# Squared-ReLU attention with expert routing: the 64-key tail tile of each chunk in one score product instead of two

## The chip, the cores and the metric

The kernel runs on one core of a Trainium2 chip. The metric is the device time of one execution in microseconds (us). The engines are PE (TensorE, matmuls; PEld is its weight load), ACT (ScalarE), DVE (VectorE), POOL (GpSimd) and SP (SyncE, which issues most DMAs). Each has its own queue of instructions; semaphores order them across engines.

## The reference, cut to what matters

```python
scores = (1.0 / S) * np.matmul(z, z.transpose(0, 2, 1))
attn = np.maximum(scores, 0.0) ** 2
x = (u * np.matmul(attn, v)).reshape(B * S, D)
# each row of x goes to one of 4 x 4 experts, chosen by two argmax steps
h = np.maximum(x_e @ w1[e], 0.0)
out = weight * (h @ w2[e])
```

B is 8 batches, S 1856 tokens, D 256 features; z has 64 features. All inputs are fp32. There are 16 experts with 1024 hidden units each.

## The kernel before, in words

**Precision.** A product of fp32 numbers is built from fp32r parts: a number is split into a rounded high part and the low rest, and high x low products are added. ACT writes the high part (a cast), DVE subtracts it from the original to get the low part. z has only 64 features, so each z tile holds z twice, in partitions 0 to 63 and 64 to 127. `z2h` is the high part of both copies, `z2l` the low part of both (`split_z`, L269; `prep_z`, L251, for later batches). The query side `zm` (`prep_zm`, L301) holds the high part in its upper 64 partitions and the low part in its lower 64. One product `z2h` x `zm` thus gives high x high + high x low, and `z2l` x `zm` gives the rest.

**Attention.** For every batch the queries come in four chunks of 512, 512, 320 and 512 columns (`QW`). A chunk has 15 key steps (`NK`): 14 full tiles of 128 keys and the tail of 64. `scores` (L342) makes the scores of one step: two products into one PSUM bank out of three (L349, L350), a Relu by ACT (L352), a square by ACT (L358), the rounding to the high part by DVE (L359) and the low part by DVE (L362). In steps 4 and 10 of a chunk (`ACT_TWICE`) ACT makes the high part with a second square instead (L355, L356). `attn_v` (L370) multiplies with the values: six products a step (L381, L382, L384), into two banks of accumulators. Scores run five steps (`LEAD`) ahead of it.

**The tail step before.** The 64 tail keys are loaded twice side by side (L279 to L281 and `prep_z`), so that `z2h` and `z2l` have 128 columns for this step and its scores stand in all 128 partitions, twice. DVE then keeps the high part in the upper 64 partitions and overwrites the lower 64 with the low part (L365); the values of the tail stand twice as well, and four products finish the step.

**After a chunk.** `chunk_end` (L392) gates with u (L402, DVE), splits the result (L403 ACT, L404 DVE), and defers the rest to later steps: `logits` (L435), four PE products for the router and a transpose by DMA; `planes` (L417), ACT copies whose 16-bit halves go through four transposes on SP into `rows`; `logits_tr` (L450). `route` (L483) is a chain of some twenty small DVE operations, three a step, which ends in a scatter of the rows to their experts by POOL. It updates `base`, the experts' fill counts (L566). The router uses a single PSUM bank (`ps_m`) for logits and for ranks.

**Loads and splits.** `PREP` (L930) says at which (chunk, step) each quarter of the next batch's v and z is loaded and at which it is split. In the last batch `E0_LOADS`, `E0_CUTS`, `E1_LOADS` and `E1_CUTS` (L934 to L937) do the same for the weights of the first two experts, in four pieces each; the last piece of expert 1 is split by `start_piece` (L1250) in the expert stage. z tiles and the logits' planes share two buffers (tag `zr`).

**Order.** The first 15 steps (`NHELD`) and the expert stage run in the order in which they are written, on PE, ACT, DVE and SP. The steps between are ordered by a planner that simulates the engines and gives each the oldest instruction that it takes to be ready; an instruction marked `held` (L186) stays behind what was traced before it on its engine. Each engine's order is fixed when the kernel is built.

**Experts.** `up` (L764) and `down` (L778) work through blocks of up to 512 rows, eight groups of products a block. The first block's products are woven into the last attention steps.

## Time and profile before

| | |
|---|---|
| median of 3 runs | 1507.86 us (1505.93 to 1508.85) |
| the profiled execution | 1506.0 us |
| its span, first to last instruction | 1504.2 us |
| PE busy | 1488.0 us, 7607 matmuls |
| DVE, ACT busy | 1102.7 us, 996.0 us |
| POOL busy | 298.6 us |
| end of attention, start of the expert stage | some 840 us into the span |

The span starts with the first instruction of the program. In rows of a timeline the first number is the start in us, the second the duration in us; a wait stands in brackets behind, with what ended it. A matmul's duration runs until its result is written and overlaps with the next ones, so that the distance of two starts is what one costs. In rows of groups the numbers behind the bar are busy time in us and the mean duration in ns, and behind the second bar the idle time of the engine just before.

### The profile page before, as it was taken

The page shows a single profiled execution, that of the slowest core. Times are in us where ns is not written, and L with a number is a line of the kernel's source. Part 1 is how long each engine was busy: PE and PEld are TensorE (multiplying, and loading weights), DVE is VectorE, ACT ScalarE, POOL GpSimd, SP SyncE. Part 2 cuts the span into 40 slices and gives each one's busy share as a digit, 9 for nine tenths or more (in the row PEclk, how much of TensorE's full clock was granted, in tenths as well). Part 3 has the DMA queues.
Part 4 walks back from the last instruction along what each step waited for, and adds up shares of the span by engine and source line. Part 5 has one row for each costly group of instructions (what it writes and reads, how often), then busy time and mean ns, then how long its engine had stood idle before and what let it go on. Part 6 is the DMA issues. An engine that isn't in the chain of part 4 may idle for free. (4 is left out here: it accounts for less than half of the span.)

```text
span 1504.2 us, 23839 instructions
## 1 busy us (share of the span) xinstructions
PE 1488.0 (99%) x7607; PEld 1297.4 (86%) x7607; DVE 1102.7 (73%) x2619; ACT 996.0 (66%) x1885; POOL 298.6 (20%) x343
## 2 busy tenths in 40 slices
PE   9999999999999999999999999999999999999997
PEld 7888888888888888888888799999888899889996
DVE  7888888888787888788798656665665556666663
ACT  8888888888888888888788435444444444444442
POOL 0012121121202121211103122321222222222222
PEclk9999999999999999999999999999999999999999
DMA  4323423333335244332574384866545665767641
GB/s 137 106 73 110 97 74 102 88 85 91 97 78 113 61 114 85 75 83 73 155 235 127 90 154 101 161 142 138 111 87 114 142 135 138 134 140 135 135 94 50
DMA packets 303588, 167.76 MB, mean 112 GB/s; under 512 B 239467, under 2 KB 282477, under 8 KB 303216
## 3 DMA queue, kind: packets, MB, share of 16 engines
q1 hardware_dynamic: 290896, 132.63, 40.5%
q0 software_dynamic: 11968, 30.91, 6.8%
q14 instruction: 277, 2.27, 0.6%
q8 instruction: 95, 1.56, 0.5%
q10 hardware_dynamic: 352, 0.39, 0.1%
HBM read 72.51 MB, written 41.60 MB: 76 GB/s over the span
## 5 line engine op out<-in xcount | busy, mean ns | idle before, releaser
L773 ACT ACTIVATE hh<-ph 128x512 fp32r<-128x512 f32 (+7 forms) x296 | 150.2, 515 | 318.1 <-PE ph L771 240.8
L381 PE MATMUL o<-ah,vl 128*128 128x512 f32 (+1 forms) x960 | 354.5, 371 | 0.6 <-DVE ah L359 0.4
L382 PE MATMUL o<-ah,vh 128*128 128x512 f32 (+1 forms) x960 | 354.4, 371 | 0.0
L774 DVE SCALAR_TENSOR_TENSOR hl<-ph,hh 128x512 fp32r<-128x512 f32 (+7 forms) x296 | 169.9, 581 | 224.3 <-ACT hh L773 213.7
L362 DVE TENSOR_TENSOR al<-r,ah 128x512 fp32r<-128x512 f32 (+1 forms) x448 | 285.5, 638 | 51.5 <-ACT r L356 42.8
L352 ACT ACTIVATE r<-sc 128x512 f32<-128x512 f32 (+1 forms) x480 | 260.1, 552 | 94.4 <-PE sc L350 69.3
L384 PE MATMUL o<-al,vh 128*128 128x512 f32 (+1 forms) x896 | 295.4, 372 | 0.0
L358 ACT ACTIVATE r<-r 128x512 f32<-128x512 f32 (+1 forms) x416 | 240.9, 592 | 6.1
L576 POOL DMA_INDIRECT bucket<-rows,di x120 | 130.4, 1087 | 538.6 <-issue 217.5
L789 POOL DMA_INDIRECT out_dram<-yf,meta x129 | 144.1, 1117 | 458.3 <-DVE yf L833 411.7
L769 PE MATMUL ph<-xh_m,w1l_e 128*128 128x512 f32 (+7 forms) x592 | 205.5, 347 | 1.3 <-issue 1.3
L771 PE MATMUL ph<-xl_m,w1h_e 128*128 128x512 f32 (+7 forms) x592 | 205.5, 347 | 0.3 <-DVE xl_m L750 0.2
L381 PEld LDWEIGHTS o<-ah,vl 128*128 128x128 f32 x960 | 180.5, 188 | 28.8 <-DVE vl L299 0.6
L770 PE MATMUL ph<-xh_m,w1h_e 128*128 128x512 f32 (+7 forms) x592 | 205.1, 346 | 0.0
L382 PEld LDWEIGHTS o<-ah,vh 128*128 128x128 f32 x960 | 180.5, 188 | 27.3
L786 PE MATMUL y<-hl,w_e 128*128 128x512 f32 (+7 forms) x576 | 200.5, 348 | 0.4 <-DVE hl L774 0.4
L784 PE MATMUL y<-hh,w_e 128*128 128x512 f32 (+7 forms) x576 | 200.1, 347 | 0.0
L785 PE MATMUL y<-hh,w_e 128*128 128x512 f32 (+7 forms) x576 | 200.0, 347 | 0.0
L359 DVE CAST ah<-r 128x512 fp32r<-128x512 f32 (+1 forms) x416 | 166.1, 400 | 37.0 <-ACT r L358 35.5
L384 PEld LDWEIGHTS o<-al,vh 128*128 128x128 f32 x896 | 165.3, 188 | 27.5 <-DVE al L362 0.4
L349 PE MATMUL sc<-zm,z2h 128*128 128x512 f32 (+1 forms) x480 | 179.9, 375 | 0.0
L350 PE MATMUL sc<-zm,z2l 128*128 128x512 f32 (+1 forms) x480 | 177.7, 371 | 0.0
(148 smaller groups left out, 2056.3 us busy)
## 6 DMA issues: line engine op xcount, KB each, us to landing
raw_e<-in_w_dram SPq DMA_DIRECT2D x64, 512.0 KB
ut<-in_uT_dram SPq DMA_DIRECT2D x24, 512.0 KB
vr<-in_v_dram SPq DMA_DIRECT2D x23, 512.0 KB
bucket<-padrow SPq DMA_DIRECT2D x16, 528.0 KB
zr<-in_zT_dram SPq DMA_DIRECT2D x47, 128.0 KB
ut<-in_uT_dram SPq DMA_DIRECT2D x8, 320.0 KB
vr<-in_v_dram SPq DMA_DIRECT2D x9, 256.0 KB
out_dram<-yf,meta POOLq DMA_INDIRECT x129, 3.2
```

The source lines that it names most:

```text
L352: nc.scalar.activation(out=a, in_=ps[:, 0:w], func=AF.Relu, scale=1.0 / S)
L358: nc.scalar.activation(out=a, in_=a, func=AF.Square)
L362: nc.vector.tensor_sub(out=al, in0=a, in1=f32(ah))
L381: nc.tensor.matmul(o, vl[:, dsl], ah, start=(k == 0), stop=False)
L382: newest[:] = [nc.tensor.matmul(o, vh[:, dsl], ah, start=False, stop=(k == NK - 1))]
L384: nc.tensor.matmul(o, vh[:, dsl], al, start=False, stop=False)
L769: nc.tensor.matmul(o, wt["l"][d][:, fs], xh[:, d, 0:W], start=(d == 0), stop=False)
L770: nc.tensor.matmul(o, wt["h"][d][:, fs], xh[:, d, 0:W], start=False, stop=False)
L771: nc.tensor.matmul(o, wt["h"][d][:, fs], xl[:, d, 0:W], start=False, stop=(d == ND - 1))
L784: nc.tensor.matmul(o, w2t[:, 1, dsl], hh[:, 0:W], start=(f == 0), stop=False)
L785: nc.tensor.matmul(o, w2t[:, 0, dsl], hh[:, 0:W], start=False, stop=False)
L786: nc.tensor.matmul(o, w2t[:, 0, dsl], hl_[:, 0:W], start=False, stop=(f == NF - 1))
```

## The change

The tail tile is no longer loaded twice. Its `z2h` columns get the high part in the first 64 and the low part, made by one more DVE subtract, in the second 64. One product with `zm` then gives partial sums in partitions 0 to 63 (from the high part) and 64 to 127 (from the low part). ACT copies the second half to partitions 0 to 63 of an SBUF tile, DVE adds the first half from PSUM, and Relu, square and rounding run on 64 partitions; the low part is written into partitions 64 to 127 from there. In the 320-wide chunk ACT now squares twice in steps 8, 10 and 12 instead of 4 and 10. The second half of the gating in `chunk_end` is deferred by a step, and the two `planes` from steps 3 and 4 to 6 and 8 behind the chunk, except in the last batch. The tables of loads and splits get other times, with one of their own for the first batch, and the third weight piece of expert 1 is split in the expert stage.

```diff
-    ACT_TWICE = (4, 10)
+    ACT_TWICE = ((4, 10), (8, 10, 12))
...
     def prep_z(b, c):
...
-        for h in range(2):
-            nc.sync.dma_start(zr[h * DQ:(h + 1) * DQ, 0:w], zT[b, :, q0:q0 + w])
-            if wx > w:
-                nc.sync.dma_start(zr[h * DQ:(h + 1) * DQ, w:wx], zT[b, :, S - TAIL:S])
...
+        load_z(b, c, zr, (nc.sync, nc.sync))
+        return lambda: split_z(b, c, zr)
 
     def split_z(b, c, zr):
...
+        w = ZW[c]
         z2h, z2l = new_z(f"z2h_{b}_{c}"), new_z(f"z2l_{b}_{c}")
...
+        ins = nc.scalar.copy(out=z2h[:, 0:w], in_=zr[:, 0:w])
+        if b > 0:
+            held(ins)
+        nc.vector.tensor_sub(out=z2l[:, 0:w], in0=zr[:, 0:w], in1=f32(z2h[:, 0:w]))
+        if c == NQ - 1:
+            tail = slice(w - TAIL, w)
+            nc.vector.tensor_sub(out=z2h[:, w:w + TAIL], in0=zr[:, tail], in1=f32(z2h[:, tail]))
...
     def load_z(b, c, zr, queues):
...
-            if c == NQ - 1:
-                queues[h].dma_start(zr[h * DQ:(h + 1) * DQ, w:w + TAIL], zT[b, :, S - TAIL:S])
...
     def scores(s):
...
-        nc.tensor.matmul(ps[:, 0:w], z2h[:, ks], zm, start=True, stop=False)
-        nc.tensor.matmul(ps[:, 0:w], z2l[:, ks], zm, start=False, stop=True)
+        nc.tensor.matmul(ps[:, 0:w], z2h[:, ks], zm, start=True, stop=k == NKF)
         a = sb("r", [P, 512], F32, 4, f"r_{s}")[:, 0:w]
-        nc.scalar.activation(out=a, in_=ps[:, 0:w], func=AF.Relu, scale=1.0 / S)
+        if k < NKF:
+            nc.tensor.matmul(ps[:, 0:w], z2l[:, ks], zm, start=False, stop=True)
+            nc.scalar.activation(out=a, in_=ps[:, 0:w], func=AF.Relu, scale=1.0 / S)
+        else:
+            a = a[0:TAIL]
+            nc.scalar.copy(out=a, in_=ps[TAIL:P, 0:w])
+            nc.vector.tensor_add(out=a, in0=ps[0:TAIL, 0:w], in1=a)
+            nc.scalar.activation(out=a, in_=a, func=AF.Relu, scale=1.0 / S)
         ah = new_z(f"ah_{s}")[:, 0:w]
-        if k in ACT_TWICE:
+        if k in ACT_TWICE[w == min(QW)]:
...
-            nc.vector.tensor_copy(out=ah, in_=a)
+            nc.vector.tensor_copy(out=ah[0:a.shape[0]], in_=a)
...
-            nc.vector.tensor_sub(out=ah[TAIL:P, :], in0=a[TAIL:P, :], in1=f32(ah[TAIL:P, :]))
+            nc.vector.tensor_sub(out=ah[TAIL:P, :], in0=a, in1=f32(ah[0:TAIL, :]))
...
     def chunk_end(s):
...
-        for d in range(ND):
+
+        def gate(d):
             nc.vector.tensor_mul(out=xT[:, d, :], in0=oa[d][:, 0:w], in1=u_t[:, d, :])
...
+        gate(0)
+        if b + 1 == B:
+            gate(1)
+        else:
+            defer(s + 1, lambda: gate(1))
...
-        defer(s + 3, lambda: planes(0))
-        defer(s + 4, lambda: planes(1))
+        defer(s + (3 if b + 1 == B else 6), lambda: planes(0))
+        defer(s + (4 if b + 1 == B else 8), lambda: planes(1))
...
     PREP = (
-        ("v", 0, (0, 1), (0, 6)), ("v", 1, (0, 7), (0, 12)), ("v", 2, (0, 13), (1, 4)), ("v", 3, (1, 5), (1, 10)),
-        ("z", 0, (1, 7), (1, 13)), ("z", 1, (2, 5), (2, 11)), ("z", 2, (3, 5), (3, 11)), ("z", 3, (3, 6), (3, 13)),
+        ("v", 0, (0, 1), (0, 5)), ("v", 1, (0, 6), (0, 11)), ("v", 2, (0, 12), (1, 3)), ("v", 3, (1, 4), (1, 7)),
+        ("z", 0, (1, 5), (1, 9)), ("z", 1, (2, 13), (3, 5)), ("z", 2, (3, 4), (3, 9)), ("z", 3, (3, 7), (3, 12)),
     )
-    E0_LOADS = ((1, 4), (1, 5), (1, 12), (2, 0))
-    E0_CUTS = ((1, 11), (1, 14), (2, 5), (2, 9))
-    E1_LOADS = ((2, 9), (2, 13), (3, 7), (3, 11))
-    E1_CUTS = ((3, 6), (3, 9), (3, 13))
+    PREP0 = (
+        ("v", 0, (0, 6), (0, 11)), ("v", 1, (0, 7), (0, 12)), ("v", 2, (0, 13), (1, 4)), ("v", 3, (1, 5), (1, 8)),
+        ("z", 0, (1, 6), (1, 10)), ("z", 1, (2, 13), (3, 5)), ("z", 2, (3, 4), (3, 9)), ("z", 3, (3, 7), (3, 12)),
+    )
+    E0_LOADS = ((1, 4), (1, 5), (1, 9), (1, 12))
+    E0_CUTS = ((1, 8), (1, 11), (1, 13), (3, 1))
+    E1_LOADS = ((2, 9), (3, 2), (3, 8), (3, 11))
+    E1_CUTS = ((3, 7), (3, 10))
...
-    def start_piece():
-        add_w(wts[1], 3, "e1")
-        e1_cuts[3]()
-
-    then(5, start_piece)
+    def start_piece(pc):
+        add_w(wts[1], pc, "e1")
+        e1_cuts[pc]()
+
+    then(3, lambda: start_piece(2))
+    then(5, lambda: start_piece(3))
```

`w == min(QW)` is true in the 320-wide chunk and picks the second entry of `ACT_TWICE`. `PREP0` is used in the first batch; `PREP` before had one exception for it, v 0 at (0, 6) and (0, 11).

## Rows read from the trace of the kernel before

**Rows 1.** The page: span, busy time by engine, and one costly group.
```profile
span 1504.2 us, 23839 instructions
...
PE 1488.0 (99%) x7607; PEld 1297.4 (86%) x7607; DVE 1102.7 (73%) x2619; ACT 996.0 (66%) x1885; POOL 298.6 (20%) x343
...
L381 PE MATMUL o<-ah,vl 128*128 128x512 f32 (+1 forms) x960 | 354.5, 371 | 0.6 <-DVE ah L359 0.4
```

**Rows 2.** Busy time by stretches of the span; the last line sums the first 850 us.
```profile
core 0: us, PE busy (x) PEld busy (x) DVE busy (x) ACT busy (x) POOL busy (x), PEclk, DMA share, GB/s
...
50.00:250.00 200.00, 200.00 (x980) 168.66 (x979) 166.74 (x480) 170.20 (x323) 33.76 (x40) 1.00 0.35 91
...
sum 850.00, PE 845.29 PEld 709.37 DVE 704.63 ACT 704.74 POOL 140.17; mean PE 120.76 PEld 101.34 DVE 100.66 ACT 100.68 POOL 20.02
```

**Rows 3.** Timeline of PE in batch 3: first and last of fifteen starts.
```profile
334.80 0.39 PE L349 MATMUL sc<-zm,z2h 128*128 128x512 f32 x1
...
337.97 0.39 PE L350 MATMUL sc<-zm,z2l 128*128 128x512 f32 x1
```

**Rows 4.** Timeline of PE, last batch: first and last of thirteen narrow starts, then scores.
```profile
798.02 0.31 PE L381 MATMUL o<-ah,vl 128*128 128x320 f32 x1
...
799.78 0.31 PE L381 MATMUL o<-ah,vl 128*128 128x320 f32 x1
...
800.37 0.39 PE L349 MATMUL sc<-zm,z2h 128*128 128x512 f32 x1
```

**Rows 5.** Groups by line and shape, ACT and DVE.
```profile
L352 ACT ACTIVATE r<-sc 128x512 f32<-128x512 f32 x360 | 210.1, 591 | 69.9 <-PE sc L350 54.5 <-DVE al L362 7.9 <-PE pk L557 1.4
...
L352 ACT ACTIVATE r<-sc 128x320 f32<-128x320 f32 x120 | 50.1, 435 | 24.5 <-PE sc L350 14.8 <-DVE al L362 8.2 <-DVE ah L365 1.4
...
L359 DVE CAST ah<-r 128x320 fp32r<-128x320 f32 x104 | 34.3, 330 | 4.9 <-ACT r L358 4.2 <-PE sc L350 0.7
...
L402 DVE TENSOR_TENSOR xT<-o,ut 128x512 f32<-128x512 f32 x48 | 31.9, 683 | 0.2
...
L402 DVE TENSOR_TENSOR xT<-o,ut 128x320 f32<-128x320 f32 x16 | 7.6, 481 | 0.0
...
L355 ACT ACTIVATE ah<-r 128x320 fp32r<-128x320 f32 x16 | 7.5, 470 | 0.0
...
L455 DVE TENSOR_TENSOR lg<-lgf 128x80 f32<-128x80 f32 x24 | 5.7, 236 | 0.2
```

**Rows 6.** Waits: who waited for whom, total us, times, longest us.
```profile
DVE al L362 <- ACT r L356: 42.8, 34, 2.4
```

**Rows 7.** Timeline of batch 3: the tail step of the 320-wide chunk.
```profile
384.12 0.31 PE L350 MATMUL sc<-zm,z2l 128*128 128x320 f32 x1
...
385.94 0.44 ACT L352 ACTIVATE r<-sc 128x320 f32<-128x320 f32 x1 [1.08 <-DVE al L362]
...
389.15 0.49 DVE L365 TENSOR_TENSOR ah<-r,ah 64x320 fp32r<-64x320 f32 x1
...
392.64 0.30 PE L381 MATMUL o<-ah,vl 128*128 128x320 f32 x1
```

**Rows 8.** Timeline around the end of attention.
```profile
830.44 0.69 DVE L214 TENSOR_TENSOR w_e<-raw_e,w_e 128x512 fp32r<-128x512 f32 x1
...
841.29 0.47 PE L438 MATMUL pl<-xh,whl 128*128 128x512 f32 x1 [2.82 <-DVE base L566]
...
842.26 1.05 ACT L748 CAST xh_m<-xf 128x1024 fp32r<-128x1024 f32 x1 [2.14 <-PE pl L438]
...
844.74 0.69 DVE L774 SCALAR_TENSOR_TENSOR hl<-ph,hh 128x512 fp32r<-128x512 f32 x1 [2.68 <-ACT hh L773]
```

**Rows 9.** Timeline of the last batch: the tail step of the 320-wide chunk.
```profile
801.11 0.35 DVE L452 COPY lgf<-lgx 128x320 uint16<-128x320 uint16 x1 [1.56 <-DMA lgx<-lgp]
...
801.49 0.49 DVE L365 TENSOR_TENSOR ah<-r,ah 64x320 fp32r<-64x320 f32 x1
...
802.05 0.40 PE L381 MATMUL o<-ah,vl 128*128 128x320 f32 x1
```

More of the change, by code (lines that the diff above doesn't have):

```diff
@@ L972, in step @@
         if b + 1 < B:
-            for what, n, load, cut in PREP:
-                if b == 0 and (what, n) == ("v", 0):
-                    load, cut = (0, 6), (0, 11)
+            for what, n, load, cut in PREP if b else PREP0:
                 if (c, k) == load:
```

12 lines of the change are left out of this document (removed).

## The prediction

> **What bounds the kernel now.** I read the page first: the profiled execution has a span of 1504.2 us and took 1506.0 us with what lies around the span; the median of the runs shown is 1507.86 us, 1.9 us above that execution. TensorE (PE) is busy for 99% of the span [rows 1], which alone proves little, since matmul ends are modelled. So I looked for waits: the product that a late split would hold up, L381, sat idle 0.6 us in all of its 960 instances [rows 1]. The view by stretches says the same of the attention stage: in each 200 us PE is busy 200.00 us at a granted clock of 1.00, ScalarE (ACT) 170 us and VectorE (DVE) 167 us [rows 2]. The timeline shows what "busy" is worth: from 334.80 to 337.97 us fifteen 512-wide products start, fourteen steps of 0.226 us without a hole [rows 3]; the 320-wide ones start every (799.78 - 798.02) / 12 = 0.147 us [rows 4]. In attention, then, PE's number of products sets the time, and the other engines have some 15% to spare. The one large hole of the stage is its end, 2.82 us [rows 8].
>
> **The products removed.** The last key tile of each chunk loses its second score product. There are 8 x 4 = 32 chunks, 24 of 512 queries and 8 of 320: 24 x 0.226 + 8 x 0.147 = 5.4 + 1.2 = **6.6 us** less on PE. Nothing lies beside these slots: PE is the engine without holes, so they come off the path whole, as long as what follows is ready in time. [...]
>
> **What the tail step gains on ACT and DVE.** ACT copies 64 partitions out of PSUM, 24 x 0.591 + 8 x 0.435 us by the Relu that reads the same bank; DVE adds the halves, 24 x 0.683 + 8 x 0.481 us by the multiply that reads PSUM and SBUF; eight 64-wide subtracts for z, at most 0.236 us each [rows 5]. I take rows on 128 partitions for work on 64: the subtract on 64 partitions takes 0.49 us for 320 columns [rows 7], the multiply on 128 takes 0.481 [rows 5]. With three doubled squares instead of two in the 320-wide chunk, ACT gets 8 x 0.470 more and DVE loses 8 x 0.330 [rows 5]. Sums: ACT 17.7 + 3.8 = +21.5 us, DVE 20.2 + 1.9 - 2.6 = +19.5 us. In the first 850 us they are busy 704.74 and 704.63 us [rows 2], so both go to some 726 of 843, 86%. Cost on the path: zero, hidden under PE. If that cover were gone, at most the 21.5 us would show.
>
> **What the tail step gains in length.** The add waits for the copy, the Relu for the add. Behind the add stand the next steps' casts and subtracts and the routing's small operations; behind the Relu the next Relus and squares; PE waits for the tail's split, and the score bank is held until the add is done. Bare, the chain grows by 0.591 + 0.683 = 1.27 us (0.92 us in the narrow chunk), and a hand-over between the two engines that is waited for costs 42.8 / 34 = 1.26 us in the mean [rows 6]. The cushion is the lead of five key steps. In the narrow chunk of batch 3 the tail's second product ends at 384.43, its split at 389.64, and PE uses it at 392.64: 3.0 us to spare, with one wait of ACT for DVE, 1.08 us, already in that road [rows 7]. So 3.0 stand against 0.92 bare, or 0.92 + 2 x 1.26 = 3.4 with two waited hand-overs, or 0.92 + 2 x 2.4 = 5.7 with two of the longest. I take zero, nearest to the bare figure, because the planner fills a wait with other work; the ends are 0 and, over eight narrow chunks, 8 x 2.7 = 21.6 us.
>
> **What is moved.** z, v and weight splits, the gating of the second half of the features and the two plane copies keep their number; each chunk's planes, and the four SyncE (SP) transposes behind them, come three and four steps later in all but the last batch, and SP's later loads of z and v with them. Splits stand four to five steps behind their loads, about 8 us at 8 x 0.226 a step, and the planner has the whole chunk after that before rows are scattered by POOL. Two small SP transfers of z per batch go. z tiles 1 and 2 and the logits' planes now meet on two buffers: tile 2's load may wait for tile 1's split one step on, and its own split is four steps further. I price all this at zero, hidden under the same PE stream, which lost 0.6 us in the whole run to late splits [rows 1]; without that cover a waited hand-over in each of seven batches would be 7 x 1.26 = 8.8 us.
>
> **The first and the last batch.** The first 15 steps are ordered by hand, so there ACT stands still for the add: between 0 and 1.27 + 1.26 = 2.5 us, taken as 0 as PE has five steps in hand. In the last batch expert weights are split too, and the cushion is gone: in its narrow chunk the tail's split, held by a DVE wait of 1.56 us for the logits' transpose, ends at 801.98 and PE uses it at 802.05 [rows 9]. The change adds 0.92 us there, but takes the first expert's splits out of that chunk. I take 0; the ends are 0 and 1.27 us for each of the batch's four tails, 5.1 us. At the end of attention PE waits 2.82 us for the routing of the chunk before last; a split of the second expert's weights, one of two of 0.69 us each, stands on DVE in front of that routing [rows 8]. Both move into the expert stage, at its fourth product group, perhaps in front of `base` again. There ACT idles 2.14 us and DVE 2.68 us [rows 8], which hides them. Ends: -2.82 (the wait goes) and 2 x 0.685 = +1.4; I take 0.
>
> **Sum.** 1506.0 - 6.6 = 1499.4 us for the profiled execution, and with the 1.9 us above it **1501.3 us** for the median.
>
> **The rivals.** *Slower: the hand-overs eat the cushion.* ACT and DVE take their work in order; a narrow tail whose copy, add and Relu wait twice for 2.4 us reaches PE 2.7 us late, in eight chunks: 1501.3 + 21.6 = 1522.9 us. It decides from 3.0 + (6.6 + 3.0) / 8 = 4.2 us of extra chain per narrow tail, where the gain and 3.0 us more are gone. For it: the waits are there [rows 6], and the last batch has no cushion [rows 9]. Against: PE's order is planned, and at 800.37 PE was given four 512-wide score products ahead of a late tail [rows 4]. [...] Chance 0.07.
>
> *No change: given back in the last batch.* +1.4 at the end of attention and +2.5 from two of the four tails: 1501.3 + 3.9 = 1505.2 us. For it: the last batch's DVE. Against: weight splits leave the narrow chunk. Chance 0.11.
>
> *No change: products do not set the pace.* If ACT and DVE drove PE, a freed slot would become a gap and the time would stay 1507.9 us. Against: starts of even spacing and 0.6 us of waits. Chance 0.05.
>
> *Less: a product is worth less than its slot.* If a 512-wide product freed only the 0.147 us of a narrow one, because its neighbours' weight loads need its cover, 32 x 0.147 = 4.7 us come off: 1503.2 us. Against: the even 0.226. Chance 0.04. [...]
>
> **How the numbers follow.** The forecast, 6.6 us off give or take the small ends, has 0.73. A measurement of this kernel tells about 0.2%, 3.0 us, from no change. Faster: 0.73 + 0.04 = 0.77; same: 0.11 + 0.05 = 0.16; slower: 0.07. The range goes from 1498.0 (the 2.82 us wait gone too, and 0.5 for the spread of runs) to 1506.0 (the last-batch rival and 0.8); outside lie the slower case, the one at 1507.9 and some 0.05 below.
>
> **What would show it.** Right: 448 instead of 480 second score products; PE still at 200.00 of 200 us; starts 0.226 us apart; the attention stage shorter by 6 to 7 us; DVE and ACT each some 20 us busier; the wait at its end between 0 and 4.2 us. Wrong: PE idle before the tail's value products, ACT waiting long for the new add in every tail step, a longer wait before the last logits, or a spacing that grows where a product went.

## The result and the profile after: slower by 0.8%

The changed kernel takes 1520.17 us (median of 6 runs, 1517.47 to 1529.44), the kernel before 1508.3 us in the runs beside it: a ratio of 1.0081 (95% interval 1.0066 to 1.0096). The forecast was 1501.3 us and its range ended at 1506.0. The profiled execution took 1520.44 us.

The page of the changed kernel, with the lines that answer to [rows 1]: the span, the engines, and two groups that idle.

```profile
span 1518.3 us, 23768 instructions
...
PE 1488.9 (98%) x7575; PEld 1295.2 (85%) x7575; DVE 1112.1 (73%) x2651; ACT 1007.8 (66%) x1925; POOL 293.5 (19%) x343
...
L772 PE MATMUL ph<-xh_m,w1l_e 128*128 128x512 f32 (+7 forms) x592 | 206.1, 348 | 4.5 <-issue 4.5
L774 PE MATMUL ph<-xl_m,w1h_e 128*128 128x512 f32 (+7 forms) x592 | 206.0, 348 | 2.4 <-DVE xl_m L753 2.4
...
L339 PE MATMUL sc<-zm,z2h 128*128 128x512 f32 (+1 forms) x480 | 181.5, 379 | 6.7 <-ACT r L343 6.3
```

The line of the kernel before that answers to L772:

```profile
L769 PE MATMUL ph<-xh_m,w1l_e 128*128 128x512 f32 (+7 forms) x592 | 205.5, 347 | 1.3 <-issue 1.3
```

32 products are gone, yet PE is not busy for less (1488.9 us against 1488.0): products at a lower clock, which come below, last longer (512-wide ones 0.63 us instead of 0.39 where the granted clock is 0.56). And idle time has appeared in front of score products (6.7 us) and in the experts' stage (4.5 us before the first product of a group, 1.3 before the change; 2.4 us before L774, which waits for split rows).

The view by stretches, with the lines that answer to [rows 2]; columns as there.

```profile
50.00:250.00 200.00, 199.59 (x973) 167.33 (x972) 171.81 (x493) 171.53 (x333) 31.90 (x39) 1.00 0.36 91
...
650.00:850.00 200.00, 191.43 (x924) 159.01 (x923) 163.86 (x476) 157.86 (x303) 29.63 (x37) 0.98 0.48 129
```

The steady stage is nearly as full as before (199.59 of 200 us); the stretch that holds the last batch is not (191.43).

To see where time goes, I cut each profiled execution into four stages by starts read from the timeline of PE: the first score product of batch 1, that of batch 7, and the 49th product of the experts' blocks, which stands just behind the end of attention. All stage lengths below are made so; in us:

| kernel | batch 0 | batches 1 to 6 | last batch | experts | median | ratio to before (95%) |
|---|---|---|---|---|---|---|
| before | 102.8 | 616.3 | 124.5 | 660.5 | 1507.86 | |
| changed | 103.8 | 613.9 | 132.4 | 668.1 | 1520.17 | 1.0081 (1.0066 to 1.0096) |

So batches 1 to 6 gain 2.4 us; batch 0 loses 1.0, the last batch 7.9 and the experts, which the change barely touches (two weight pieces instead of one are split there), 7.6. Of these 7.6 us, 5.4 are idle time of PE: 3.2 in issue waits and 2.2 in waits for split rows.

**The hole in the last batch.** The timeline of the changed kernel, SP, ACT, DVE and PE at the start of its narrow chunk; a wait stands in brackets.

```profile
765.51 6.18 SPq L431 DMA_TRANSPOSE rows<-pl  x4
...
772.59 1.64 SPq L449 DMA_TRANSPOSE lgx<-lgp  x1
776.43 0.95 SPq L197 DMA_DIRECT2D raw_e<-in_w_dram  x2
...
780.04 1.04 ACT L201 CAST w1h_e<-raw_e 128x1024 fp32r<-128x1024 f32 x1 [7.30 <-DMA raw_e<-in_w_dram]
...
781.00 0.59 ACT L343 ACTIVATE r<-sc 128x512 f32<-128x512 f32 x1
...
781.12 1.23 DVE L202 TENSOR_TENSOR w1l_e<-raw_e,w1h_e 128x1024 fp32r<-128x1024 f32 x1 [7.17 <-ACT w1h_e L201]
...
781.64 0.63 PE L339 MATMUL sc<-zm,z2h 128*128 128x320 f32 x1 [5.89 <-ACT r L343]
...
784.02 0.63 PE L377 MATMUL o<-ah,vl 128*128 128x512 f32 x1
784.45 0.63 PE L378 MATMUL o<-ah,vh 128*128 128x512 f32 x1
```

The same places in the kernel before:

```profile
763.09 6.82 SPq L428 DMA_TRANSPOSE rows<-pl  x4
770.01 1.21 SPq L446 DMA_TRANSPOSE lgx<-lgp  x1
772.88 1.20 SPq L197 DMA_DIRECT2D raw_e<-in_w_dram  x2
...
777.86 1.03 ACT L201 CAST w1h_e<-raw_e 128x1024 fp32r<-128x1024 f32 x1
```

Read it from the bottom up: PE waits 5.89 us for a Relu, the Relu stands on ACT behind the first split of expert 0's weights (L201), and that split waits 7.30 us for a load which SP issues only at 776.43, behind four row transposes and one of logits. The load was written four key steps ahead of the split, but in the kernel before, too, it left SP 24 us after its chunk's first score product (772.88 after 748.6); after the change it is 31 us (776.43 after 745.6). Scores run further ahead after the change; counted from the first value product of the step at which the load is written (763.93 and 761.86 us), the load leaves 9.0 us later before the change and 14.6 after it. Before, the split stood three key steps later, and there was no wait. Behind the hole 512-wide products start 0.43 us apart instead of 0.226 [rows 3], and the granted clock (PEclk) from 782 to 786 us is 0.56, behind 5.89 us in which PE stood.

```profile
782.00:786.00 4.00, 3.53 (x10) 2.56 (x10) 4.00 (x11) 2.81 (x6) 0.00 (x0) 0.56 1.08 329
```

ACT works through its queue in order here: it stands 7.30 us for the load of the split at its head, and the Relu that PE waits for starts behind that split, at 781.00.

### The profile page after: what moved, and what is told of

Read it like the earlier page. It is cut to its first block, busy times and chain, and to the rows that moved or that the text cites. A ratio compares the mean times of both kernels' runs of the same rounds, so it can differ in the third digit from the quotient of the medians.

```text
span 1518.3 us, 23768 instructions
## 1 busy us (share of the span) xinstructions
PE 1488.9 (98%) x7575; PEld 1295.2 (85%) x7575; DVE 1112.1 (73%) x2651; ACT 1007.8 (66%) x1925; POOL 293.5 (19%) x343
## 3 DMA queue, kind: packets, MB, share of 16 engines
q14 instruction: 275, 2.25, 0.6%
## 4 chain that ended last, share of the span: by engine, by line
PE 84%; DVE 5%; issue 4%; DMA 3%; SPq 2%; ACT 1%; POOL 0%; DVEq 0%; POOLq 0%; ACTq 0%
PE o L377 12%; PE o L378 12%; PE o L380 11%; PE ph L772 6%; PE ph L774 6%; PE ph L773 6%; PE y L789 6%; PE y L787 6%; PE y L788 6%; PE sc L339 6%; PE sc L342 5%; PE pl L441 1%; DMA out_dram<-yf,meta 1%; DVE al L358 1%; PE pl L442 1%
## 5 line engine op out<-in xcount | busy, mean ns | idle before, releaser
L343 ACT ACTIVATE r<-sc 128x512 f32<-128x512 f32 (+1 forms) x448 | 241.9, 552 | 63.1 <-PE sc L342 36.3
L380 PE MATMUL o<-al,vh 128*128 128x512 f32 (+1 forms) x896 | 268.4, 373 | 1.7 <-DVE al L358 1.7
L354 ACT ACTIVATE r<-r 128x512 f32<-128x512 f32 (+3 forms) x408 | 234.5, 590 | 3.9
L579 POOL DMA_INDIRECT bucket<-rows,di x120 | 124.6, 1038 | 558.8 <-issue 255.2
L772 PE MATMUL ph<-xh_m,w1l_e 128*128 128x512 f32 (+7 forms) x592 | 206.1, 348 | 4.5 <-issue 4.5
L774 PE MATMUL ph<-xl_m,w1h_e 128*128 128x512 f32 (+7 forms) x592 | 206.0, 348 | 2.4 <-DVE xl_m L753 2.4
L355 DVE CAST ah<-r 128x512 fp32r<-128x512 f32 (+3 forms) x408 | 161.5, 401 | 17.5 <-ACT r L354 16.4
L342 PE MATMUL sc<-zm,z2l 128*128 128x512 f32 (+1 forms) x448 | 166.0, 371 | 0.0
## 6 DMA issues: line engine op xcount, KB each, us to landing
zr<-in_zT_dram SPq DMA_DIRECT2D x47, 128.0 KB
```

What stands on the lines that cost most here:

```text
L342: nc.tensor.matmul(ps[:, 0:w], z2l[:, ks], zm, start=False, stop=True)
L380: nc.tensor.matmul(o, vh[:, dsl], al, start=False, stop=False)
L772: nc.tensor.matmul(o, wt["l"][d][:, fs], xh[:, d, 0:W], start=(d == 0), stop=False)
L774: nc.tensor.matmul(o, wt["h"][d][:, fs], xl[:, d, 0:W], start=False, stop=(d == ND - 1))
```

## The experiments

"Theory" numbers are those of the expectations. Every kernel was timed beside the kernel before, whose medians there lie between 1507.7 and 1508.9 us, so that two medians from different groups compare to about 1.3 us. The table at the end of this section gives all stages.

### The split that was moved ahead: E1, E2, E4

E1, the changed kernel with the first expert's table of before:

```diff
-    E0_LOADS = ((1, 4), (1, 5), (1, 9), (1, 12))
-    E0_CUTS = ((1, 8), (1, 11), (1, 13), (3, 1))
+    E0_LOADS = ((1, 4), (1, 5), (1, 12), (2, 0))
+    E0_CUTS = ((1, 11), (1, 14), (2, 5), (2, 9))
```

> The changed kernel with the loads and splits of the first expert's weights (E0_LOADS, E0_CUTS) at their old steps, all else as changed. Theory 1 (the first split, moved three steps forward, holds ACT until its weights have come through SP's queue; the 7.3 us wait of ACT and the 6.3 us hole of PE behind it are the loss): both vanish, 8 to 10 us come off, 1510 to 1512 us. Theory 2 (the longer chain of the tail step, 32 times, eats the gain): nothing comes off, 1518 to 1521 us.

Measured: 1511.72 us, 1.0029 (1.0019 to 1.0040). Its timeline:

```profile
775.59 0.95 SPq L197 DMA_DIRECT2D raw_e<-in_w_dram  x2
...
779.13 1.05 ACT L201 CAST w1h_e<-raw_e 128x1024 fp32r<-128x1024 f32 x1 [1.46 <-DMA raw_e<-in_w_dram]
```

The load is hardly earlier (775.59), but the split now waits 1.46 us instead of 7.30. 8.5 us come back with two lines of a table, as theory 1 said: in the profiles 4.4 in the last batch (132.4 to 128.0) and 3.5 in the experts' stage (668.1 to 664.6). 4 us of loss are left.

E2, the kernel before with all new weight tables (first and second expert, and the second late piece), nothing else:

```diff
-    E0_CUTS = ((1, 11), (1, 14), (2, 5), (2, 9))
+    E0_CUTS = ((1, 8), (1, 11), (1, 13), (3, 1))
...
+    then(3, lambda: start_piece(2))
```

> The kernel before with only the last batch's new weight tables (E0, E1 and the piece moved into the expert stage); two score products as before, nothing else moved. Theory 1: the wait of ACT for the first weights comes back in the old kernel, 1508 + 8 to 10 = 1516 to 1518 us. Theory 2: no tail chain, so no loss, 1507 to 1510 us.

Measured: 1510.54 us, 1.0021 (1.0012 to 1.0030), between the two theories and near the second.

```profile
776.12 1.05 ACT L201 CAST w1h_e<-raw_e 128x1024 fp32r<-128x1024 f32 x1 [2.61 <-DMA raw_e<-in_w_dram]
```

The load leaves SP at 772.66 us, as in the kernel before, and ACT waits 2.61 us for it, not 7.30. The tables alone cost a third of what E1 got back.

E4, the changed kernel with the old two-product tail, so that only the moves are left:

```diff
-        nc.tensor.matmul(ps[:, 0:w], z2h[:, ks], zm, start=True, stop=k == NKF)
+        nc.tensor.matmul(ps[:, 0:w], z2h[:, ks], zm, start=True, stop=False)
+        nc.tensor.matmul(ps[:, 0:w], z2l[:, ks], zm, start=False, stop=True)
```

> The changed kernel with the old tail (z tail loaded twice, two products, no copy and no add); all moves in time stay. Theory 1: the loss stays and the gain of 3 to 6.6 us is missing, 1522 to 1527 us. Theory 2: without the tail's chain the loss goes, 1510 us or less.

Measured: 1520.8 us, 1.0092 (1.0078 to 1.0106), as slow as the whole change and just below theory 1's range. Its timeline has the hole, with the load even later:

```profile
778.72 0.98 SPq L197 DMA_DIRECT2D raw_e<-in_w_dram  x2
...
782.02 1.04 ACT L201 CAST w1h_e<-raw_e 128x1024 fp32r<-128x1024 f32 x1 [5.45 <-DMA raw_e<-in_w_dram]
...
783.61 0.63 PE L349 MATMUL sc<-zm,z2h 128*128 128x320 f32 x1 [3.83 <-ACT r L352]
```

So the long wait needs both: the split in front (E1 takes that away), and a queue of SP that has become later. With the split in front alone the wait is 2.61 us (E2, where the load leaves 9.0 us behind the first value product of its step, as before). The other moves alone make the queue later (E4, 14.1 us), and the hole does not need the new tail. But the moves are not the only thing that makes it later: in E3, next, where no table has moved, it is 14.3 us.

### The tail alone: E3

The kernel before with the one-product tail and nothing moved (old tables, gating, planes and doubled squares):

```diff
-        for h in range(2):
-            nc.sync.dma_start(zr[h * DQ:(h + 1) * DQ, 0:w], zT[b, :, q0:q0 + w])
...
+        load_z(b, c, zr, (nc.sync, nc.sync))
...
+        if k < NKF:
+            nc.tensor.matmul(ps[:, 0:w], z2l[:, ks], zm, start=False, stop=True)
```

> The kernel before with only the one-product tail (z tail loaded once, low part beside the high part, halves added across partitions); every time in the tables, the doubled squares, gating and planes as before. Theory 1: the removed products come off with little given back, 6.6 us off and up to 3 us given back: 1501.7 to 1505 us. Theory 2: the hand-overs of the tail step cost more than the products: 1510 us or more.

Measured: 1525.65 us, 1.0113 (1.0097 to 1.0129), the slowest of all: theory 2's time. Batches 1 to 6 gain 0.5 us, the last batch loses 12.2. Its timeline in that batch:

```profile
778.37 0.95 SPq L197 DMA_DIRECT2D raw_e<-in_w_dram  x2
...
813.88 0.17 DVE L753 TENSOR_TENSOR meta<-meta,none 128x4 int32<-128x4 int32 x1 [4.34 <-DMA meta<-bucket]
...
814.69 0.73 PE L380 MATMUL o<-al,vh 128*128 128x512 f32 x2 [2.66 <-DVE al L358]
...
840.34 1.14 ACT L213 CAST w_e<-raw_e 128x512 fp32r<-128x512 f32 x2 [4.53 <-DMA raw_e<-in_w_dram]
...
843.05 0.50 PE L377 MATMUL o<-ah,vl 128*128 128x512 f32 x1 [2.29 <-DVE ah L361]
```

Here it is another instruction, a small DVE operation for the first expert's rows, that was put in order before its DMA landed: DVE stands for 4.34 us and PE for 2.66. At the end of the batch PE waits 2.29 us for the split of the last tail, one of the prediction's signs of being wrong; but that split stands on DVE behind weight splits whose load ACT waits 4.53 us for, so that theory 2's mechanism, the hand-overs, is not what these two waits show. Tail alone -0.5, moves alone +1.2 (E4), both together -2.4 us in batches 1 to 6: the moves seem to make the room that the tail needs there. The moves of gating and planes are not among those that do, since E8 and E11, without them, gain 2.9 and 3.1 us.

### The experts: E7, and E9 to E12

The idle time in front of the experts' first products is put down to "issue", at entries of the branches into an expert's code (in the changed kernel the longest COMPARE_BRANCH of PE, 5.65 us, ends 0.15 us before the product at 1182.51, whose wait is 1.85 us). The kernels with one-product tails had it at other products than the kernel before. PE's program is shorter in them. The expectations count 32 instructions for the change, one for each product; but with each product a weight load goes too (both counts on the page fall by 32), and PE has 15 semaphore waits more. As traced, PE runs 8236 instructions up to the 49th product of the experts before the change and 8187 after it, 49 fewer. E7 is the kernel before with 16 fewer warm products (each is a weight load and a matmul; both counts on its page fall by 16, to 7591), 32 instructions shorter:

```diff
-    NWARM = 46
+    NWARM = 30
```

> The kernel before with 30 instead of 46 warm products ahead of the first score: PE's program is as many instructions shorter as the change makes it (32), and nothing else differs. Theory 3 (the place of PE's code decides which branches into the expert stage's arms wait): issue waits at the 186th, 270th and 1902nd product of the expert stage instead of the 402nd and 462nd, and an expert stage 2 to 3 us longer, 1510 us. Rival (the waits at branches come from what the one-product tail does to the router or the experts' counts, or from the last batch): issue waits stay at the 402nd and 462nd, 1507.5 to 1508.5 us.

Measured: 1511.25 us, 1.0022 (1.0008 to 1.0036), runs from 1508.39 to 1518.42 us (17 runs of before beside it: 1506.94 to 1513.31 us). Its profiled execution took 1515.04 us: attention is as long as before, the experts take 669.3 us instead of 660.5. So theory 3's main point holds, waits that grow with nothing changed but the length (7.1 us of issue waits instead of 1.3); of the three places that it named only the 270th product has one (the others are the 402nd and the 1038th, counted from 0 as there). Its page has, for the first product of a group:

```profile
L769 PE MATMUL ph<-xh_m,w1l_e 128*128 128x512 f32 (+7 forms) x592 | 206.6, 349 | 7.1 <-issue 7.1
```

The timeline of PE at the longest of these waits:

```profile
886.87 0.28 PE L786 MATMUL y<-hl,w_e 128*128 128x256 f32 x1
...
890.79 0.40 PE L769 MATMUL ph<-xh_m,w1l_e 128*128 128x288 f32 x1 [3.65 <-issue]
```

The view by stretches around it (columns as in [rows 2]):

```profile
880.00:886.00 6.00, 6.00 (x52) 6.00 (x51) 3.02 (x6) 3.94 (x8) 1.80 (x2) 1.00 1.10 234
886.00:891.00 5.00, 1.35 (x11) 1.16 (x10) 1.31 (x3) 0.38 (x1) 0.35 (x1) 1.00 1.63 126
891.00:894.00 3.00, 3.00 (x18) 3.00 (x18) 0.39 (x2) 0.41 (x1) 0.18 (x1) 0.66 1.15 146
894.00:900.00 6.00, 6.00 (x44) 6.00 (x44) 4.76 (x11) 2.71 (x7) 3.39 (x3) 0.88 0.30 70
```

Two views of the DMA queues: the kernel before from 50 to 850 us, and E7 from 886.9 to 887.0 us (packets, MB, the time of the packets as a share of 16 engines):

```profile
q8 instruction: 30, 0.49, 0.3%
...
q8 instruction: 1, 0.02, 140.9%
```

PE waits for nothing that the profile shows. The profile has two instruction queues, q8 and q14, and does not say for which engine they load. In the first view q8 moves 30 packets of 16 KiB while PE runs 3892 matmuls and 3891 weight loads, some 260 a packet. In the hole one packet of q8 starts as PE stops and takes 140.9% x 16 x 0.1 = 2.25 us, and PE starts 1.6 us after its end. The kernels have 20 issue waits of 0.8 us or more in front of the experts' products; in 19 of them the last packet of q8 ends 1.5 to 1.7 us before PE starts, and in one of E10's 2.2 us. The packets of q14 come at no such fixed distance (in the changed kernel's two longest such waits the last one ends 0.2 and 5.9 us before PE starts). From these distances I take the wait to be for PE's own next instructions; no run tests it in another way.

The hole of 3.65 us costs more than itself: the granted clock is 0.66 and 0.88 in the stretches behind it, and compared product by product the kernel falls 4.9 us behind the one before here.

E9 to E12 put most of the length of PE's program back in four kernels: 62 (E12: 60) warm products of 64 columns instead of 46 of 128. The expectations call this the old length; as traced, E9 and E10 stay 17 instructions short of the kernel before, E12 15 and E11 12.

```diff
-    NWARM = 46
+    NWARM = 62
...
-            nc.tensor.matmul(wps[:, 0:P], ones, ones, start=True, stop=True)
+            nc.tensor.matmul(wps[:, 0:64], ones, ones[:, 0:64], start=True, stop=True)
```

E9 is the changed kernel with this edit alone.

> The changed kernel with 62 warm products of 64 columns ahead of the first score instead of 46 of 128: PE's program is as long as before the change, so the code of the expert stage lies where it lay in the kernel before. Theory 3 (the place of PE's code makes the waits of PE at the entries of the expert arms): issue waits in front of the first up product (4.5 us in the changed kernel, 1.3 before, 7.1 in the kernel before with the shorter program) fall to 1 to 2 us, the expert stage from the 48th product on takes 661 to 664 us instead of 668, and the time is 1513 to 1516 us. Rival (the longer expert stage comes from late data, splits or row transposes, that the change causes): the stage stays at 667 to 668 us and the time at 1519 to 1521 us. The last batch stays at some 132 us in both.

Measured: 1517.82 us, 1.0059 (1.0044 to 1.0074). The experts take 662.9 us in its profile instead of 668.1, as theory 3 said; the last batch keeps its hole (133.9 us), and the time is 1.8 us above theory 3's range. Its page:

```profile
L772 PE MATMUL ph<-xh_m,w1l_e 128*128 128x512 f32 (+7 forms) x592 | 205.6, 347 | 2.4 <-issue 2.4
```

E10 is E1 with the edit.

> The first run's kernel (first expert's split at its old steps) with the same 62 warm products. Theory 3: the expert stage goes from 664.6 to 660 to 662 us, the rest stays, 1507 to 1509 us, level with the kernel before: what is left of the 6.6 us is then lost in the last batch (128 against 124.5 us) alone. Rival: 1511 to 1512 us.

Measured: 1511.98 us, 1.0017 (1.0004 to 1.0031): nothing gained in the median. Its runs lie between 1507.41 and 1518.73 us, and its profile, an upper one (1513.11 us), has 5.0 us of issue waits. Nearly the old length does not rule the waits out. A miss for theory 3 in its simple form, though not at the very length: the three kernels within one instruction of it (before, E2 and E4) have 1.0 to 1.4 us.

### Gating and planes: E8 and E11

E8 is E1 with the gating and the plane copies at their old steps:

```diff
-        if b + 1 == B:
-            gate(1)
-        else:
-            defer(s + 1, lambda: gate(1))
+        gate(1)
...
-        defer(s + (3 if b + 1 == B else 6), lambda: planes(0))
-        defer(s + (4 if b + 1 == B else 8), lambda: planes(1))
+        defer(s + 3, lambda: planes(0))
+        defer(s + 4, lambda: planes(1))
```

> The changed kernel with the first expert's table of before (as in the first run) and with the gating and the plane copies at their old steps too. Theory 4 (the later plane copies and gating make the router's chain late, which costs PE the 0.46 us wait for base in each of the batches 1 to 6): the wait before the logits goes and a batch takes 101.9 to 102.0 us instead of 102.37, the time 1508 to 1509.5 us. Rival (the tail step's own DVE and ACT work makes the chain late): the wait for base stays at 0.4 to 0.6 us a batch, 1511 to 1512.5 us. In both, SP issues the last batch's weight loads as late as in the first run.

Measured: 1515.14 us, 1.0044 (1.0028 to 1.0060), above both ranges, with 4.3 us of issue waits in its profile. E11 is the same with the 62 warm products.

> The kernel with the first expert's table, the gating and the planes of before, with the same 62 warm products. Theory 3: its profile's expert stage goes from 665.5 to 660 to 662 us and the spread of its runs (1511.9 to 1518.0) narrows to some 3 us, 1506 to 1509 us. Rival: 1512 to 1516 us with the same spread.

Measured: 1506.66 us, 0.9993 (0.9981 to 1.0005), level with the kernel before and in theory 3's range; 0.9 us of issue waits. The spread did not narrow to 3 us (1504.77 to 1511.24). Between E8 and E11 only warm products differ, and 8.5 us of the medians.

In the steady batches theory 4 holds for the wait, not for the time. The changed kernel's timeline, batch 4, and the same place in E16 (below), which has the old gating and planes:

```profile
480.70 0.31 PE L342 MATMUL sc<-zm,z2l 128*128 128x320 f32 x1
481.39 0.47 PE L441 MATMUL pl<-xh,whl 128*128 128x512 f32 x1 [0.38 <-DVE base L569]
```
```profile
479.01 0.17 PE L564 MATMUL pk<-pre,ones 128*128 128x16 bf16 x1
479.50 0.42 PE L343 MATMUL sc<-zm,z2h 128*128 128x320 f32 x1 [0.31 <-ACT r L347]
```

In the changed kernel PE starts 0.69 us after a product whose slot is 0.147 [rows 4], so 0.54 us of the 0.83 that a batch gains (3 x 0.226 + 0.147) go to the router's `base`. With gating and planes back that wait is gone, and in its place PE waits for a score bank that a Relu still reads. From batch 4 to batch 5 the three kernels take 102.73 (before), 102.37 and 102.46 us. E8 and E11, with the old gating and planes too, take 101.93 and 101.91, the whole gain of a batch, and 103.49 and 102.69 in the next.

### The last batch: E5, E6, E12, E13, E15

E5 is E1 with the second expert's table of before too, and one late weight piece instead of two.

```diff
-    E1_LOADS = ((2, 9), (3, 2), (3, 8), (3, 11))
-    E1_CUTS = ((3, 7), (3, 10))
+    E1_LOADS = ((2, 9), (2, 13), (3, 7), (3, 11))
+    E1_CUTS = ((3, 6), (3, 9), (3, 13))
```

> The changed kernel with all tables of the last batch's weight splits as before (both experts, and one late piece instead of two). Theory 1 (the last batch's loss is weight splits put in order ahead of their weights): the last batch loses what the first run left (128.0 against 124.5 us) too, 1508 to 1510 us. Theory 3 (what is left of the loss lies in the expert stage and comes from PE's shorter program): the last batch comes to 125 to 126 us, the expert stage keeps its 2 to 3 us of issue waits at the 186th, 270th and 1902nd product, 1509 to 1511 us. Theory 2 (the longer chain of the tail step in the last batch is the rest): no change from the first run, 1511 to 1512 us.

Measured: 1520.26 us, 1.0072 (1.0058 to 1.0086). None of the three: the last batch is 4 us longer than in E1. The second expert's new table was a part that helped.

E6 has the changed batches 0 to 6, and the last batch with all its own parts as before (two-product tails, tables); E12 is the same with 60 warm products.

```diff
-        nc.tensor.matmul(ps[:, 0:w], z2h[:, ks], zm, start=True, stop=k == NKF)
+        single = k == NKF and b + 1 < B
+        nc.tensor.matmul(ps[:, 0:w], z2h[:, ks], zm, start=True, stop=single)
```

> Batches 0 to 6 as changed; the last batch with two products per tail, doubled tail keys and all weight tables of before. Theory 2 (in the last batch the longer tail chain meets an engine without slack): the last batch is back at 124 to 125 us, batches 0 to 6 keep their 1.5 to 2.4 us of gain, 1506 to 1507 us where the expert stage keeps its length, 1508 to 1509 with the 2 to 3 us of issue waits that went with the shorter PE program. Theory 1 (weight splits alone): the same as the kernel with all weight tables back, within 1 us.

> Batches 0 to 6 as changed, the last batch as before, with 60 warm products of 64 columns so that PE's program is as long as before. Theory 3: the expert stage goes from 668.2 to 660 to 662 us; the last batch stays at 128 us (its waits for splits and for the experts' base do not depend on PE's code), 1508 to 1510 us. Rival: 1514 to 1516 us.

Measured: E6 1515.69 us, 1.0048 (1.0032 to 1.0063), E12 1510.59 us, 1.0009 (0.9999 to 1.0019). The experts' stage of E12 is as theory 3 said; E6 has neither theory's time. The last batch took 128.1 and 126.5 us, not 124.5, though nothing of its own had changed. E13 is E12 with the old gating and planes; E15 is E11 with the second expert's table of before, and so differs from E13 in the last batch's four tails and their doubled squares.

> One-product tails in batches 0 to 6 alone; the last batch, the weight tables, the gating and the planes as before; 60 warm products of 64 columns, so that PE's code lies where it did. Theory 5 (batch 6's late planes are what the last batch still lost, 126.5 against 124.5 us, when everything of its own was as before): the last batch is back at 124 to 125 us, batches 1 to 6 stay at 613.4 us, the expert stage at 660 to 662 us, 1503.5 to 1505.5 us, below the kernel before. Rival (the new times of loads and splits of batch 6, or the place of other engines' code, cost the last batch its 2 us): 126 to 127 us, 1506 to 1507 us.

> One-product tails in all eight batches, with the weight tables, the gating and the planes of before; 62 warm products of 64 columns. Against the first kernel of this call only the four tails of the last batch differ. Theory 2 (in the last batch, where ACT and DVE also split weights, the longer tail chain makes PE wait): the last batch takes 128 to 132 us instead of 124 to 125, with waits of the tail's value products for DVE, 1508 to 1512 us. Rival (the last batch's tails cost nothing, its loss is the weight tables and what batch 6 leaves): the last batch within 0.5 us of the first kernel's, the time within 1 us of it.

Measured: E13 1509.54 us, 1.0003 (0.9993 to 1.0013); E15 1512.14 us, 1.0024 (1.0013 to 1.0034). Theory 5 falls, and its rival with it: with batch 6's planes back in time the last batch was 129.5 us, longer than in E12. Theory 2 gets 1.0 us in the profiles (130.5 against 129.5) and 2.6 in the medians, outside its rival's bounds, but PE waits for no tail's split in E15's last batch. E13's timeline shows what paces its end:

```profile
830.70 0.43 DVE L459 COPY lgf<-lgx 128x240 uint16<-128x240 uint16 x1 [2.67 <-DMA lgx<-lgp]
...
843.88 0.77 PE L445 MATMUL pl<-xh,whl 128*128 128x512 f32 x1 [3.97 <-DVE df L576]
```

That is the wait of [rows 8], 2.82 us before, now 3.97 (0.98 in E11 and E16). As I read it, the chain from the last but one chunk's logits through a transpose by DMA and the router on DVE is not shortened by products that PE saves, and where it starts is the planner's choice.

### The first batch, and the best that came out: E14, E16 to E18

E14 is E13 with batch 0 as before too (`single = k == NKF and b not in (0, B - 1)`, and the old table as `PREP0`). E16 is E11 with batch 0 as before; E17 and E18 are E16 with 76 and 92 warm products instead of 60.

> The same with batch 0 and its table of loads and splits as before too, so that one-product tails stand in batches 1 to 6 alone; 58 warm products. Theory 6 (the tail step's longer hold of the score bank costs the hand-ordered first batch about 1 us, 103.8 against 102.8): batch 0 at 102.8 to 103.1 us, the rest as in the kernel beside it, 1502.5 to 1504.5 us, the fastest of all. Rival (the 1 us comes from the start, the warm products or the splits, not from the tails): 103.6 to 103.9 us, 1503.5 to 1505.5 us.

> The kernel with the first expert's table, the gating and the planes of before, one-product tails in batches 1 to 7 and batch 0 (tails, table of loads and splits) as before; 60 warm products of 64 columns keep PE's code in its place. Theory 6 (the tail step costs the hand-ordered first batch 1.4 us): batch 0 at 102.5 us instead of 103.9, batches 1 to 6 at 613.2 to 613.6, the last batch to the 48th expert product at 126 to 127, the expert stage at 660.5 to 662, 1504.5 to 1506 us, the lowest of all. Rival (a faster first batch moves the same wait into a later one, as the last batch did with the gain of batches 1 to 6): 1506 to 1508 us.

Measured: E14 1511.14 us, 1.0014 (1.0003 to 1.0024), outside both ranges; E16 1505.89 us, 0.9997 (0.9988 to 1.0006), in theory 6's. For batch 0 theory 6 holds in both: it takes 102.5 us instead of 104.0 and 103.9. That this is the tails and not the table, which goes back with them, is shown by E4 and E3: the new table with old tails has 102.7 us, the old table with new tails 104.6. In the changed kernel's first batch the score bank is indeed held by the new add:

```profile
33.28 0.50 PE L339 MATMUL sc<-zm,z2h 128*128 128x512 f32 x1 [0.41 <-DVE r L347]
```

Yet in E16 the last batch is 1.2 us longer than in E11, so most of it is given back. E16 has the lowest median of all kernels, and the comparison cannot tell it from the kernel before.

> The same with 76 warm products: PE's program is 32 instructions longer than before the change. Theory 3 (the place of PE's code sets which entries of expert arms wait): the issue waits in front of the first up product stand at other products than the 186th, 402nd and 462nd, or have other lengths, and the expert stage moves by 1 to 8 us either way; batch 0 gets 0 to 1.3 us longer by the warm products. Rival (only the shorter program hurts): the expert stage within 1 us of the first kernel's.

> The same with 92 warm products, PE's program 64 instructions longer than before the change. Theory 3: issue waits at other products again, the expert stage 1 to 8 us from the first kernel's in at least one of the two longer programs; batch 0 gets 0 to 2.6 us longer. Rival: within 1 us in both.

Measured: E17 1507.82 us, 1.0002 (0.9993 to 1.0011), E18 1508.34 us, 1.0007 (0.9998 to 1.0016); issue waits 0.0 and 0.4 us, and E17's page has

```profile
L776 PE MATMUL ph<-xh_m,w1l_e 128*128 128x512 f32 (+7 forms) x592 | 205.4, 347 | 0.0
```

As traced, they run 22 and 54 instructions more than the kernel before, and E16 10 fewer. The experts take 662.3 and 659.6 us against E16's 658.8, E17's 3.5 us in good part by other, smaller waits (3.9 us of idle time of PE in the stage against 1.7), so that theory 3's length came out there but not its mechanism. These two longer programs have next to no issue waits; their medians are 1.9 and 2.5 us above E16's, which stays unexplained. What stands is narrower than theory 3: the seven kernels that are 32 to 50 instructions short have 3.1 to 7.1 us of issue waits, the eight that are 8 to 17 short 0.2 to 5.0, the five others 0.0 to 1.4.

| kernel | batch 0 | 1 to 6 | last batch | experts | median | ratio (95%) |
|---|---|---|---|---|---|---|
| E1 first split back | 103.5 | 613.5 | 128.0 | 664.6 | 1511.72 | 1.0029 (1.0019 to 1.0040) |
| E2 new tables alone | 102.6 | 616.3 | 127.6 | 661.3 | 1510.54 | 1.0021 (1.0012 to 1.0030) |
| E3 tail alone | 104.6 | 615.8 | 136.7 | 666.8 | 1525.65 | 1.0113 (1.0097 to 1.0129) |
| E4 moves alone | 102.7 | 617.5 | 134.8 | 662.4 | 1520.80 | 1.0092 (1.0078 to 1.0106) |
| E5 all tables back | 103.6 | 613.9 | 132.1 | 666.9 | 1520.26 | 1.0072 (1.0058 to 1.0086) |
| E6 last batch as before | 103.4 | 614.6 | 128.1 | 668.2 | 1515.69 | 1.0048 (1.0032 to 1.0063) |
| E7 before, shorter program | 102.6 | 616.4 | 124.8 | 669.3 | 1511.25 | 1.0022 (1.0008 to 1.0036) |
| E8 E1, gating, planes back | 103.8 | 613.4 | 127.4 | 665.5 | 1515.14 | 1.0044 (1.0028 to 1.0060) |
| E9 changed, 62 warm products | 103.8 | 614.2 | 133.9 | 662.9 | 1517.82 | 1.0059 (1.0044 to 1.0074) |
| E10 E1, 62 warm products | 103.7 | 614.0 | 129.4 | 664.0 | 1511.98 | 1.0017 (1.0004 to 1.0031) |
| E11 E8, 62 warm products | 103.9 | 613.2 | 126.2 | 661.4 | 1506.66 | 0.9993 (0.9981 to 1.0005) |
| E12 E6, 60 warm products | 103.7 | 614.1 | 126.5 | 660.6 | 1510.59 | 1.0009 (0.9999 to 1.0019) |
| E13 E12, gating, planes back | 104.0 | 614.0 | 129.5 | 662.8 | 1509.54 | 1.0003 (0.9993 to 1.0013) |
| E14 E13, batch 0 back | 102.5 | 613.5 | 128.6 | 661.8 | 1511.14 | 1.0014 (1.0003 to 1.0024) |
| E15 E11, second table back | 104.0 | 613.0 | 130.5 | 660.9 | 1512.14 | 1.0024 (1.0013 to 1.0034) |
| E16 E11, batch 0 back | 102.5 | 613.6 | 127.4 | 658.8 | 1505.89 | 0.9997 (0.9988 to 1.0006) |
| E17 E16, 76 warm products | 102.4 | 613.5 | 128.6 | 662.3 | 1507.82 | 1.0002 (0.9993 to 1.0011) |
| E18 E16, 92 warm products | 102.6 | 613.6 | 129.3 | 659.6 | 1508.34 | 1.0007 (0.9998 to 1.0016) |

Stages are of one profiled execution each, and the runs of one kernel lie up to 12.0 us apart (those of the changed kernel, 1517.47 to 1529.44), so that a stage says more than a median only where it is read with its waits.

## Why the prediction was wrong, step by step

**What is moved.** This is the step that failed most. It took the moved splits at zero because "Splits stand four to five steps behind their loads, about 8 us". That counts from where the load is written to where the split is written. The load does not leave there: in SP's rows it stands behind four row transposes and one of logits, and it left 9.0 us after the first value product of its step before the change, more than those 8 us, and 14.6 after it. The row for it stands in the trace of before (772.88 us), and the text does not use it. Price: 8.5 us between the medians (E1 against the changed kernel), of which the profiles put 4.4 in the last batch and 3.5 in the experts' stage. The planes, which the text counted as free too, are not by themselves what makes the load late: with gating and planes back (E8, E11) it still leaves 13.7 and 13.6 us after that product.

**The first and the last batch.** Taken at 0 with ends of 2.5 and 5.1 us. Batch 0 cost 1.0 us, and 1.4 to 1.5 us come back when its tails and table do (E14, E16): inside the ends, and the mechanism named there, a stand for the add in a hand-ordered batch, shows in one wait of 0.41 us only. For the last batch the text feared the tails and counted the first expert's earlier splits as a relief; in the changed kernel the first split was the harm, and the four tails are worth some 1.0 us in the profiles (E15 against E13). With the tails alone and no split moved, though, the last batch loses 12.2 us (E3), far beyond the end of 5.1; two of its holes, 2.66 and 2.29 us, stand behind operations that waited for a DMA, not for the tails' hand-overs. The wait at the end of attention went from 2.82 to 0.41 us, and was paid for by the hole ahead of it.

**The products removed.** The slots are gone as worked out: 448 second score products, starts 0.23 us apart in the steady stage. But 6 batches of 0.83 us are 4.95 us, and 2.4 arrived. Of the rest, 1.75 us are idle time of PE in these batches, which had none before; 1.15 of it are three waits for `base`. The argument that nothing lies beside a slot holds for PE alone: the router's chain and the score banks stand close behind, and each freed slot turned in part into a wait for them (the rows of batch 4). The rival "products do not set the pace" was given 0.05; half of it came true.

**What the tail step gains in length.** Right. The narrow tail of batch 3 in the changed kernel, answering to [rows 7]:

```profile
384.13 0.31 PE L339 MATMUL sc<-zm,z2h 128*128 128x320 f32 x1
...
386.94 0.47 DVE L347 TENSOR_TENSOR r<-sc,r 64x320 f32<-64x320 f32 x1
...
390.62 0.48 DVE L361 TENSOR_TENSOR ah<-r,ah 64x320 fp32r<-64x320 f32 x1
...
392.80 0.31 PE L377 MATMUL o<-ah,vl 128*128 128x320 f32 x1
```

From the end of the product to the end of the split are 6.66 us instead of 5.21, 1.45 more, between the 0.92 and 3.4 of the text; 1.70 of the 3.0 us of cushion are left. The other narrow tails have 1.6 to 3.2 us left, and no wait of PE in the changed kernel ends with a tail's split. So the slower rival came out with nearly its time (1522.9 against 1520.2 us) by luck and not by its mechanism: the narrow tails did not eat the cushion.

**What the tail step gains on ACT and DVE.** The groups of the changed kernel, against the bounds of [rows 5]:

```profile
L347 DVE TENSOR_TENSOR r<-sc,r 64x512 f32<-64x512 f32 x24 | 16.3, 678 | 0.1
...
L346 ACT COPY r<-sc 64x512 f32<-64x512 f32 x24 | 14.0, 585 | 7.9 <-DVE al L358 6.7 <-PE sc L339 0.5
...
L347 DVE TENSOR_TENSOR r<-sc,r 64x320 f32<-64x320 f32 x8 | 3.8, 476 | 0.0
...
L346 ACT COPY r<-sc 64x320 f32<-64x320 f32 x8 | 3.4, 423 | 3.4 <-DVE al L358 2.2 <-DVE zm L299 0.7 <-issue 0.4
```

678 and 476 ns for 683 and 481, 585 and 423 for 591 and 435: these operations on 64 partitions took within 3% of what like ones on 128 took. Added up instruction by instruction, ACT has 19.3 and DVE 20.9 us more, close to the 21.5 and 19.5 of the text; the page, which counts overlapping instructions once, shows 11.8 and 9.4 more, not the 20 that the text looked for there. That these engines had room in the mean was true and did not help, since what PE waited for, 5.89 us in the last batch, stood behind one split at the head of ACT's queue.

**The sum** lacked a term: that the experts' stage might change with the length of PE's program. It stands in no rival. E7, with 32 of the 49 instructions gone, prices it at 2.9 us in the medians (1511.25 against 1508.37 beside it); E8 against E11, with 32 warm-product instructions between them, gives 8.5.

**What stays open.** The last batch was between 126.2 and 136.7 us in every kernel in which anything around it had changed, and 124.5 to 124.8 only in the kernel before and E7, where nothing had. In the profiles shown here ACT or DVE stands for a DMA, and not always the same one: weights (the changed kernel, E1, E2, E4), weights and the rows' numbers (E3), the logits (E13). That its order is planned anew each time, from estimates of DMA times that are off by several us (the waits for a DMA are 1.46 to 7.30 us), fits all of them; no run tried a plan with measured times, so it is argued and not shown. Nor is it shown what makes SP's queue later with the tail alone. Nor was it tried at exactly the old length of PE's program, or where the expert arms lie relative to the packets of q8.

## What to carry to other kernels

Before moving an instruction that stands in a fixed order, read when its data's DMA is issued and lands in the trace, not how many steps ahead the load is written; then ask what else is pushed in front of that load by the same edit. A pinned instruction that is early by one DMA stops its whole engine, and the engines behind it: here ACT for 7.30 us and PE for 5.89. And when an edit changes the number of instructions of an engine that branches later, change the number alone as a control before explaining a difference in a stage that the edit does not touch.

## What was not expected of the hardware

Sixteen warm products fewer at the start made the experts, 800 us later, up to 8.8 us longer (660.5 to 669.3 in the profiles), with waits of up to 3.65 us at a branch, in which a packet of 16 KiB came on the instruction queue q8; the medians differ by 2.9 us. In 19 of 20 such waits PE started 1.5 to 1.7 us after the end of that packet. And the hole of 3.65 us cost more than its length: 4.9 us, with a granted clock of 0.66 in the 3 us behind it.
